# A gated linear attention with an ELU layer: scores, states and values of two half units in two groups of products per unit

## The chip, the core and the metric

The kernel runs on one core of a Trainium2 chip. A core has a matrix engine (TensorE; PE in the profile, PEld for its weight loads), a vector engine (VectorE, DVE), an activation engine (ScalarE, ACT), a general engine (GpSimd, POOL) and a queue that mostly issues transfers (SyncE, SP). [...] The metric is the device time of one execution in microseconds, and lower is better.

## What is computed

A gated linear attention with a complex gate (4 sequences, 8 heads, 768 positions, 48 features per head) is followed by a two-layer network of width 2048 with ELU. All of it is fp32. Cut to what matters:

```python
for t in range(S):                     # S_re, S_im: one D x D state per head
    new_re = ar * S_re - ai * S_im     # ar, ai: the gate, its size capped at 0.999
    new_im = ar * S_im + ai * S_re
    S_re, S_im = new_re + k[t] v[t]^T, new_im
    y[t] = q[t] @ S_re
x = y, heads side by side              # (3072, 384)
h = x @ w_in                           # (3072, 2048)
g = where(h > 0, h, exp(min(h, 0)) - 1)
out = g @ w_out                        # (3072, 384)
```

## The kernel before

**Units.** The work is cut into 12 units. Unit `u` has 128 positions of two sequences; each of the two is a half unit `n`. Units `u` and `u + 2` continue the same two sequences, so states travel from `u` to `u + 2`. A half unit has two chunks `c` of 64 positions.

**Attention of a unit.** Logarithms and angles of the gate are summed along the positions by matmuls (`quartered`, L883, for sizes; `turned`, L832, for angles). Their exponentials, sines and cosines scale `q` and `k` (`gated`, L988). From there, for each half unit:

- `transposed` (L1003, L1004) turns `q` and `k` with TensorE, eight full-size matmuls each, through two banks of tag `w`; ScalarE copies them out to `qt` and `kt`.
- `scores` (L1011, L1016) multiplies `kt` and `qt` of each head and chunk into one `w` bank, and VectorE masks the result into `a`.
- `states` (L1039, L1049, L1051) multiplies `k` and `v` of each head and chunk into a `w` bank per chunk. For each chunk VectorE adds the old state, and GpSimd multiplies by the chunk's decay; the second chunk's sum starts from the first chunk's result.
- `values` (L1061, L1068) multiplies `v` by the masked scores, adds the product of the carried state with `qt`, both into the two-bank tile `y`, and ScalarE copies that to `x` and `y` (L1076, L1080).

`seam` then issues six small transfers from GpSimd's queue (L1093), which move the last rows of `y` into `x`. The products of scores, states and values are small: they fill a part of TensorE's 128x128 array (128x64, 64x64, 128x48 in the profile), several at a time in different places.

**Network of a unit.** `hidden` runs eight times per unit: `inner` (L1113) has twelve matmul instructions of 256 columns into a bank of tag `mlp`; `elu` (L1122 to L1124) needs two ScalarE instructions and one on VectorE. `folded` (L1197) forms sums of `g` on VectorE, four instructions for each half of the hidden width. `product` (L1219) runs 14 times per unit with eight matmul instructions of 192 columns each, into three `mlp` banks, and replaces a plain matmul with `w_out` by seven products of halves.

**PSUM.** Three banks have tag `w`, three have tag `mlp`, and the tile `y` has the last two.

**Order.** The program writes the order of the work itself. `put(at, fn, ...)` gives each step a place `at`; the steps are sorted by it, and steps of equal place stay in the order of the calls, so earlier units come first. Every engine sees its instructions in that one order. With `r = 16 (u - 2)`, these steps surround the change:

| Place | Step |
|---|---|
| r+20 to r+27 | `hidden` 0 to 7 of unit u-1; `folded` of u-1 at r+23 and r+27 |
| r+22 to r+31 | transposes, scores, states, values and seam of unit u |
| r+27 | `squares` (ScalarE, L709, L710), `joined` (GpSimd, L716) of u+1; then `test` (VectorE, L680) |
| r+28 | `logarithms`, `powers` of u+1 (ScalarE, L735 to L747) |
| r+28 to r+35.4 | the 14 products of u-1, 0.57 apart |
| r+29.4, r+29.5 | `lengths` (VectorE, L772), `ratios` (GpSimd, L759, L760) of u+1 |
| r+30.9, r+31 | `slopes` (VectorE, L780), `decays` with `quartered` of u+1 |
| r+31.5, r+32.6, r+34 | `angles` (ScalarE, L815), `carried` (VectorE, L821), `turns` with `turned` (TensorE, L832) of u+1 |

For the units from the fifth on (u of 4 and more), the last row of `values_of`'s places is, for half unit 0: q at r+22, k at r+23, scores at r+24, states at r+25, values at r+27; for half unit 1: q at r+26, k at r+27, scores at r+28, states at r+29, values at r+30; seam at r+31. The first units follow a list that is written out by hand.

Of the kernel before, what the change touches and what calls it, by code (L numbers as in the profile page):

```python
# [10 lines left out]
FP32 = mybir.dt.float32  # L11
U32 = mybir.dt.uint32
AF = mybir.ActivationFunctionType
ALU = mybir.AluOpType
PSUM = bass.MemoryType.PSUM

C = 128
L = 64
# [487 lines left out]
def kernel(  # L506
# [12 lines left out]
    nc = tc.nc  # L519
    B, H, S, D = q.shape  # L520
    DM, DF = moe_w_in.shape[0], moe_w_out.shape[0]
    NI, NF = DM // C, DF // C
    NP = H // 2
    HD = H * D
    NB = 2
    NU = B // NB * (S // C)
    GT = NB * C
# [9 lines left out]
    ps = ctx.enter_context(tc.tile_pool(name="ps", bufs=1, space=PSUM))  # L537
# [10 lines left out]
    def const(n, m, name):  # L548
        return cst.tile([n, m], FP32, name=name)
# [8 lines left out]
    G = HP - D  # L558
# [12 lines left out]
    def work(shape, tag="w"):  # L571
        return ps.tile(shape, FP32, tag=tag, bufs=3, name=tag)


    nat = [{} for _ in range(NU)]

    def where(u):
        return u % (B // NB) * NB, u // (B // NB) * C
# [114 lines left out]
    def new(tag, bufs=1, shape=None):  # L693
        return sb.tile(shape or [C, NB, H, D], FP32, tag=tag, bufs=bufs, name=tag)
# [296 lines left out]
            )  # L991


    state = {}

    def transposed(u, key, n):
        x = nat[u]
        x[key + "t", n] = o = new(key + "t", 1 + (key == "q"), [C, H, C])
        for h0 in range(0, H, 4):
            t = work([C, 4, C])  # L1000
            for h in range(4):
                of = gates[key][:, n, h0 + h].rearrange("p i d -> p (i d)")
                nc.tensor.transpose(t[:, h], of, ident)  # L1003
            nc.scalar.copy(out=o[:, h0 : h0 + 4], in_=t)  # L1004
# [13 lines left out]
        )  # L1018

    def states(u, n):  # L1020

        x = nat[u]
        b, s = where(u)
        x["S", n] = [state.get(b + n)]
        if s == S - C:
            last = C // L - 1
        else:
            last = C // L
        gs = [
            work([C, H, D], "w" if u else "mlp") for c in range(last)  # L1030
        ]
        for h in range(H):
            for c, g in enumerate(gs):
                k = gates["k"][ts(c, L), n, h]
                parts = [(g[ts(i, HP), h], k[:, i]) for i in range(2)]
                if u == 0:
                    parts = [(g[:, h], k.rearrange("p i d -> p (i d)"))]
                for to, of in parts:
                    nc.tensor.matmul(  # L1039
                        to, lhsT=of, rhs=vn[u % 2][ts(c, L), n, ts(h, D)], start=True, stop=True,  # L1040
                    )
        for c, g in enumerate(gs):
            old = x["S", n][-1]
            new_s = new("S", 8, [C, H, D])
            wide = x["T"][:, n, c].unsqueeze(2).to_broadcast([C, H, D])
            if old is None:
                nc.vector.tensor_tensor(out=new_s, in0=g, in1=wide, op=ALU.mult)
            else:
                nc.vector.tensor_tensor(out=new_s, in0=g, in1=old, op=ALU.add)  # L1049
                eng = nc.vector if u < 2 else nc.gpsimd  # L1050
                eng.tensor_tensor(out=new_s, in0=new_s, in1=wide, op=ALU.mult)  # L1051
            x["S", n].append(new_s)
        state[b + n] = x["S", n][-1]

    def values(u, n):
        x = nat[u]
        y = ps.tile([C, C // L, 512], FP32, tag="y", bufs=1, name="y")
        each = [(p, c, j) for p in range(NP) for c in range(C // L) for j in range(2)]
        for p, c, j in each:

            nc.tensor.matmul(  # L1061
                y[ts(j, HP), c, ts(p, L)], lhsT=vn[u % 2][ts(c, L), n, ds((2 * p + j) * D, HP)],
                rhs=x["a", n][ts(c, L), 2 * p + j], start=(p == 0), stop=False,
                skip_group_check=True,
            )
        for p, c, j in each:
            if x["S", n][c] is not None:
                nc.tensor.matmul(  # L1068
                    y[ds(j * HP, D), c, ts(p, L)], lhsT=x["S", n][c][:, 2 * p + j],
                    rhs=x["qt", n][:, 2 * p + j, ts(c, L)], start=False, stop=False,  # L1070
                    skip_group_check=True,
                )
        if n == 0:
            x["x"], x["y"] = new("x", 2, [C, NI, GT]), new("y", 1, [C, GT])

        nc.scalar.copy(  # L1076
            out=x["x"][:, :, ts(n, C)].rearrange("p x (c t) -> p c x t", c=C // L),
            in_=y[:, :, 0 : NI * L].rearrange("p c (x t) -> p c x t", x=NI),
        )
        nc.scalar.copy(  # L1080
            out=x["y"][:, ts(n, C)].rearrange("p (c t) -> p c t", c=C // L),
            in_=y[:, :, NI * L : NP * L],
        )

    def seam(u):
# [167 lines left out]
    def verdict():  # L1253
# [31 lines left out]
        out=ident, in_=ident, pattern=[[-1, C]], base=0, channel_multiplier=1,  # L1285
# [6 lines left out]
    sum_turns, mask = const(C, C, "sum_turns"), const(C, L, "mask")  # L1292
# [14 lines left out]
    parts = [("in", m) for m in range(NF // 2)] + [("out", m) for m in range(NF // WF)]  # L1307
# [20 lines left out]
    def put(at, fn, *args):  # L1328
        if fn is hidden:
            plan.append((at, len(plan), inner, args))  # L1330
            plan.append((at, len(plan), elu, args))
        else:
            plan.append((at, len(plan), fn, args))

    def decays_of(u, *at):
        fns = squares, logarithms, powers, lengths, ratios, slopes, noted, angles, carried
        put(at[0], begun, u)
        for x, fn in zip(at, fns):
            put(x, fn, u)
            if fn is squares:  # L1340
                put(x, joined, u)

    def gates_of(u, *at):
        for x, fn in zip(at, (decays, turns, waves, scaled, ends, gated)):
            put(x, fn, u)

    def values_of(u, *at):
        fns = (transposed, "q"), (transposed, "k"), (scores,), (states,), (values,)
        for n in range(NB):
            for x, (fn, *key) in zip(at[5 * n :], fns):  # L1350
                put(x, fn, u, *key, n)
        put(at[-1], seam, u)
# [12 lines left out]
        (scaled, 0, "k", 1), (scaled, 0, "q", 1), (warm, 1), (gated, 0, 0), (warm, 1), (noted, 0),  # L1365
        (table, "natural_log"), (warm, 2), (gated, 0, 1), (warm, 2), *3 * [(convert,)],
        (transposed, 0, "k", 0), (transposed, 0, "q", 1), (carry_on, 0), (transposed, 0, "q", 0),
        *4 * [(convert,)], (scores, 0, 0), (transposed, 0, "k", 1), (scores, 0, 1), (load_a, 1),
        (squares, 1), (joined, 1), (fetch, "in", 3), (logarithms, 1), (states, 0, 0),
        (values, 0, 0), (powers, 1), (convert,), (states, 0, 1), (lengths, 1), (load_qk, 1),  # L1370
        (convert,), (ratios, 1), (values, 0, 1), (seam, 0), (warm, 2), (warm, 2), (decays, 1),
        (load_a, 2), (warm, 1), (inner, 0, 0), *2 * [(convert,)], (noted, 1), (scaled, 1),
        (warm, 2), (convert,), (load_v, 1), (slopes, 1), (ends, 1), *3 * [(convert,)],
# [43 lines left out]
    def layer_of(u, at_h, at_p):  # L1417
        for m in range(NF // 2):
            put(at_h[m], hidden, u, 2 * m)
        put(at_h[3], folded, u, 0)  # L1420
        put(at_h[7], folded, u, 1)
        ks = [(1, 0), (4, 0), (1, 1), (4, 1)] + [(k, h) for k in (6, 5, 7, 2, 3) for h in range(2)]
        for m, (k, h) in enumerate(ks):
            put(at_p[0] + m * len(at_p) / len(ks), product, u, k, h)

    for u in range(2, NU):
        r = (u - 2) * SLOTS
        put(r + 8, load_a, u)
        put(r + 8, load_v, u)
        put(r + 8, load_qk, u)  # L1430
        if u == 2:
            decays_of(u, 16, 17, 17, 18.4, 19.5, 19.6, 22.7, 19.8, 19.8)
            gates_of(u, 20.4, 21.6, 22.1, 22.4, 22.4, 22.6)
        else:
            decays_of(u, r + 11, r + 12, r + 12, r + 13.4, r + 13.5, r + 14.9, r + 16.7, r + 15.5, r + 16.6)
            gates_of(u, r + 15, r + 18, r + 18.5, r + 18, r + 18, r + 19.5)
        values_of(u, *(max(r + 22, 24.5) + x for x in (0, 1, 2, 3, 5, 4, 5, 6, 7, 8, 9)))
        layer_of(u, range(r + 36, r + 44), range(r + 44, r + 52))
    for m in range(NR):
        put(40 + 4 * m, test_fetch, m)  # L1440
# [42 lines left out]
```

## Time and profile before

| What | Value |
|---|---|
| Time, median of 3 runs | 700.34 us (698.58 to 700.38) |
| Span of the profiled execution, first to last instruction | 700.0 us |
| Busy: TensorE, its weight loads | 674.0 us (96%), 580.5 us (83%) |
| Busy: VectorE, ScalarE, GpSimd | 389.3 us (56%), 398.5 us (57%), 197.3 us (28%) |
| `inner`, all matmuls (L1113) | 262.9 us busy |
| Scores, states (L1011, L1039) | 27.8 us, 25.8 us busy |
| Values, carried part (L1061, L1068) | 17.1 us, 25.1 us busy |
| One unit to the next, by the start of `turned` | 53.5 us (383.7 to 437.2 us) |

The profile shows one execution. Its span lies 0.3 us under the median of the timed runs and inside their spread, so a sum against the span can be read against the median with that shift. [...] neighbours overlap. What a group of matmuls costs is therefore read from its first start to the first start of the next group. A line of the timeline gives start, length, engine, line of code, operation, output and inputs, the part of the array, the shape and the count; in brackets stands the engine's idle time before it and who ended it.

### The profile page before, as it was taken

To read this page: it belongs to the slowest core of one execution; us is meant where nothing else is said; L and a number is where in the kernel's file an instruction comes from. 1 tells how busy PE (TensorE), PEld (TensorE's weight loads), DVE (VectorE), ACT (ScalarE), POOL (GpSimd) and SP (SyncE) were. 2 spreads that over 40 slices of the span, in tenths; PEclk is the share of its full clock that TensorE was granted. 3 is DMA by queue.
4 is the path that set the end of the run, shared out by engine and by line. 5 is a ranking of instruction groups with operands and counts; after the bars stand their busy time and mean duration, and the time that the engine had idled before them with its cause. 6 is when DMAs were issued, how large, how long until landed. Compare 5 with 4: busy or idle time off the path is not lost.

```text
span 700.0 us, 15771 instructions
## 1 busy us (share of the span) xinstructions
PE 674.0 (96%) x6656; PEld 580.5 (83%) x6656; DVE 389.3 (56%) x579; ACT 398.5 (57%) x630; POOL 197.3 (28%) x207
## 2 busy tenths in 40 slices
PE   8799899997999999999999999999999999999996
PEld 6687786575788889888988989889888988989995
DVE  5888999814757544554553553553554644642151
ACT  6774445748656764765655656657557547541230
POOL 2000000115514414414415415406407305402000
PEclk9979999999999999999999999999999999999999
DMA  9995756152082911821921821831731631100000
GB/s 169 175 150 83 144 176 165 17 103 64 3 137 63 143 50 38 138 43 50 136 48 53 123 61 52 121 63 53 108 75 53 123 62 52 47 1 8 23 1 28
DMA packets 149899, 55.98 MB, mean 80 GB/s; under 512 B 129172, under 2 KB 142652, under 8 KB 149820
## 3 DMA queue, kind: packets, MB, share of 16 engines
q1 hardware_dynamic: 146240, 53.53, 40.6%
q0 software_dynamic: 3360, 1.22, 1.3%
q8 instruction: 54, 0.88, 0.5%
q14 instruction: 25, 0.20, 0.1%
q10 hardware_dynamic: 220, 0.14, 0.1%
HBM read 48.88 MB, written 4.78 MB: 77 GB/s over the span
## 4 chain that ended last, share of the span: by engine, by line
PE 85%; DVE 4%; SPq 3%; ACT 2%; DMA 2%; issue 2%; POOL 1%; ACTq 0%; POOLq 0%; DVEq 0%
PE mlp L1113 33%; PE mlp L1219 26%; PE w L1003 5%; PE mlp L1134 4%; PE w L1011 3%; PE y L1068 3%; PE w L1039 3%; SPq L596 2%; PE y L1061 2%; PE w L832 2%; PE w L1134 1%; PE w L883 1%; DMA w<-in_moe_w_in_dram 1%; DMA w<-in_a_im_dram 1%; POOL kg L988 1%
## 5 line engine op out<-in xcount | busy, mean ns | idle before, releaser
L1113 PE MATMUL mlp<-x,w_in 128*128 128x256 f32 x1152 | 262.9, 383 | 2.9 <-DVE g L1124 2.9
L1113 PEld LDWEIGHTS mlp<-x,w_in 128*128 128x128 f32 x1152 | 215.8, 191 | 32.5 <-DVE g L1124 3.3
L1124 DVE SCALAR_TENSOR_TENSOR g<-ee,mlp 128x512 f32<-128x512 f32 x96 | 65.6, 685 | 116.6 <-ACT ee L1123 111.0
L1122 ACT ACTIVATE ee<-mlp 128x512 f32<-128x512 f32 x96 | 57.3, 596 | 127.6 <-PE mlp L1113 118.7
L1219 PE MATMUL mlp<-w_out,g 128*128 128x192 f32 x640 | 111.1, 328 | 0.0
L1219 PEld LDWEIGHTS mlp<-w_out,g 128*128 128x128 f32 x640 | 104.3, 190 | 2.8
L1051 POOL TENSOR_TENSOR S<-S,T 128x384 f32<-128x384 f32 x36 | 29.9, 831 | 163.7 <-DVE S L1049 163.7
L1123 ACT ACTIVATE ee<-ee 128x512 f32<-128x512 f32 x96 | 60.5, 630 | 2.9
L1197 DVE TENSOR_TENSOR g<-g 128x512 f32<-128x512 f32 x80 | 56.8, 711 | 2.7
L1219 PE MATMUL mlp<-w,g 128*128 128x192 f32 x320 | 56.9, 332 | 0.0
L1219 PEld LDWEIGHTS mlp<-w,g 128*128 128x128 f32 x320 | 51.6, 190 | 5.8 <-issue 4.8
L856 POOL DMA_DIRECT2D carry<-n x10 | 5.0, 501 | 142.0 <-DVE n L840 142.0
L988 POOL TENSOR_TENSOR kg<-k,cs 128x1536 f32<-128x1536 f32 x9 | 38.8, 4309 | 18.4 <-issue 18.4
L1093 POOL DMA_DIRECT2D x<-y x65 | 31.8, 496 | 42.7 <-ACT y L1080 42.7
L1049 DVE TENSOR_TENSOR S<-w,S 128x384 f32<-128x384 f32 x38 | 21.1, 556 | 40.7 <-PE w L1039 25.4
L893 ACT ACTIVATE n<-w 64x384 f32<-64x384 f32 (+1 forms) x60 | 28.1, 486 | 22.7 <-PE w L883 22.0
L1238 ACT COPY o<-mlp 128x192 f32<-128x192 f32 x10 | 3.2, 319 | 64.6 <-DMA out_dram<-o 42.9
L716 POOL TENSOR_TENSOR n<-n 128x768 f32<-128x768 f32 x9 | 16.4, 1819 | 66.9 <-ACT n L710 66.9
L1134 PE MATMUL mlp<-w_out,g 128*128 128x384 f32 x96 | 32.9, 490 | 0.7 <-DVE g L1124 0.7
L1004 ACT COPY qt<-w 128x512 f32<-128x512 f32 x48 | 25.5, 584 | 11.9 <-PE w L1003 11.9
L1011 PEld LDWEIGHTS w<-qt,kt 128*64 128x64 f32 x768 | 24.4, 137 | 7.9 <-issue 4.5
L988 DVE TENSOR_TENSOR qg<-q,cs 128x1536 f32<-128x1536 f32 (+1 forms) x12 | 19.5, 1623 | 19.2 <-ACT cs L966 19.2
(165 smaller groups left out, 992.3 us busy)
## 6 DMA issues: line engine op xcount, KB each, us to landing
w<-in_moe_w_out_dram SPq DMA_DIRECT2D x8, 768.0 KB
g<-in_moe_w_in_dram SPq DMA_DIRECT2D x16, 384.0 KB
g<-in_moe_w_out_dram SPq DMA_DIRECT2D x16, 384.0 KB
w<-in_moe_w_in_dram SPq DMA_DIRECT2D x16, 288.0 KB
vn<-in_v_dram SPq DMA_DIRECT2D x24, 192.0 KB
out_dram<-o SPq DMA_DIRECT2D x48, 96.0 KB
ar<-in_a_re_dram SPq DMA_DIRECT2D x22, 192.0 KB
ai<-in_a_im_dram SPq DMA_DIRECT2D x22, 192.0 KB
```

The source lines that it names most:

```text
L988: eng.tensor_tensor(out=to[:, :, :, 0:D], in0=each.unsqueeze(2).to_broadcast([C, step * H, 2, D]), in1=x["cs"][:, n * H : (n + step) * H], ...
L1003: nc.tensor.transpose(t[:, h], of, ident)
L1011: nc.tensor.matmul(t[ts(c, L), h], lhsT=x["kt", n][:, h, ts(c, L)], rhs=x["qt", n][:, h, ts(c, L)], start=True, stop=True,)
L1051: eng.tensor_tensor(out=new_s, in0=new_s, in1=wide, op=ALU.mult)
L1093: eng.dma_start(out=x["x"][ds(j * HP + D, G), i], in_=x["y"][ds(j * HP + i * G, G)])
L1113: nc.tensor.matmul(t[:, e], lhsT=w_in[:, i, ts(f + e, C)], rhs=x["x"][:, i], start=(i == 0), stop=(i == NI - 1),)
L1122: nc.scalar.activation(out=e, in_=t, func=AF.Relu, scale=-1.0)
L1123: nc.scalar.activation(out=e, in_=e, func=AF.Exp, scale=-1.0)
L1124: nc.vector.scalar_tensor_tensor(out=x["g", f // 8][:, f % 8 : f % 8 + 2], in0=e, scalar=-1.0, in1=t, op0=ALU.add, op1=ALU.max)
L1134: nc.tensor.matmul(x["o", n], lhsT=x["g", f // 8][:, f % 8, ts(n, C)], rhs=w_out[:, f], start=(f == 0), stop=(f == NF - 1),)
L1197: nc.vector.tensor_tensor(out=S_of(u, k, h), in0=a, in1=b, op=op)
L1219: nc.tensor.matmul(to, lhsT=a[:, m], rhs=b[:, m], start=(first and h == 0 and m == 0), stop=False, skip_group_check=True,)
```

## The change

From the fifth unit on, the six separate steps (scores, states, values, for two half units) become two. `states` is split into `state_products` (TensorE) and `state_sums` (VectorE and GpSimd), and `values` into `value_products`, `carried_products` and `value_copies`. The first four units keep the old order.

- `scored`, at r+26.6: the state products of half unit 0, then the scores of both half units into a tile of tag `y` (one bank for each half unit), then the sums of half unit 0 and the two masks, alternating.
- `valued`, at r+29.3: the state products of half unit 1, the value products of both half units into one tile `y` (the half units side by side in each chunk's bank), the sums of half unit 1, the carried products of both half units sorted by chunk, and three copies in place of four.
- `seam` follows at r+29.3. The transposes stand at r+22 (q, 0), r+23 (k, 0), r+24 (q, 1) and r+25.3 (k, 1). The second `kt` lies in the buffer of tag `cs`.

```diff
+    PAIRED = 4
     def transposed(u, key, n):
         x = nat[u]
-        x[key + "t", n] = o = new(key + "t", 1 + (key == "q"), [C, H, C])
+        if u >= PAIRED and key == "k" and n:
+            o = new("cs", 1, [C, H, C])
+        else:
+            o = new(key + "t", 1 + (key == "q"), [C, H, C])
+        x[key + "t", n] = o
...
+    def carried_products(u, n, y):
+        x = nat[u]
+        for p, c, j in EACH if u < PAIRED else sorted(EACH, key=lambda x: x[1]):
...
+    def scored(u):
+
+        x = nat[u]
+        state_products(u, 0)
+        t = ps.tile([C, NB, 512], FP32, tag="y", bufs=1, name="y")
+        for n in range(NB):
+            for h in range(H):
+                for c in range(C // L):
+                    nc.tensor.matmul(
+                        t[ts(c, L), n, ts(h, L)], lhsT=x["kt", n][:, h, ts(c, L)],
+                        rhs=x["qt", n][:, h, ts(c, L)], start=True, stop=True,
+                    )
+        for n in range(NB):
+            state_sums(u, 0, [n])
+            x["a", n] = new("a", 2, [C, H, L])
+            nc.vector.tensor_tensor(
+                out=x["a", n], in0=t[:, n].rearrange("p (h t) -> p h t", h=H),
+                in1=mask.unsqueeze(1).to_broadcast([C, H, L]), op=ALU.mult,
+            )
+
+    def valued(u):
+
+        x = nat[u]
+        y = ps.tile([C, C // L, 512], FP32, tag="y", bufs=1, name="y")
+        state_products(u, 1)
+        for n in range(NB):
+            value_products(u, n, y[:, :, ts(n, NP * L)], n == 0)
+        state_sums(u, 1)
+        for n in range(NB):
+            carried_products(u, n, y[:, :, ts(n, NP * L)])
+        x["x"], x["y"] = new("x", 2, [C, NI, GT]), new("y", 1, [C, GT])
+        parts = y.rearrange("p c (n x t) -> p c n x t", n=NB, x=NP)
+        to = x["x"].rearrange("p x (n c t) -> p c n x t", n=NB, c=C // L)
+        for c in range(C // L):
+            nc.scalar.copy(out=to[:, c], in_=parts[:, c, :, 0:NI])
+        nc.scalar.copy(
+            out=x["y"].rearrange("p (n c t) -> p c n t", n=NB, c=C // L), in_=parts[:, :, :, NI],
         )
...
-        values_of(u, *(max(r + 22, 24.5) + x for x in (0, 1, 2, 3, 5, 4, 5, 6, 7, 8, 9)))
+        if u < PAIRED:
+            values_of(u, *(max(r + 22, 24.5) + x for x in (0, 1, 2, 3, 5, 4, 5, 6, 7, 8, 9)))
+        else:
+            for n in range(NB):
+                put(r + 22 + 2 * n, transposed, u, "q", n)
+                put(r + 23 + 2.3 * n, transposed, u, "k", n)
+            put(r + 26.6, scored, u)
+            put(r + 29.3, valued, u)
+            put(r + 29.3, seam, u)
```

More of the change, by code (lines that the diff above doesn't have):

```diff
@@ L1020, in states, with state_products @@
     def states(u, n):
+        state_products(u, n)
+        state_sums(u, n)
+    def state_products(u, n):
         x = nat[u]
@@ L1028, in states @@
             last = C // L
-        gs = [
+        x["G", n] = gs = [
             work([C, H, D], "w" if u else "mlp") for c in range(last)
@@ L1041, in states, with state_sums @@
                     )
-        for c, g in enumerate(gs):
+    def state_sums(u, n, chunks=range(C // L)):
+        x = nat[u]
+        for c, g in list(enumerate(x["G", n])):
+            if c not in chunks:
+                continue
             old = x["S", n][-1]
@@ L1052, in states, with value_products @@
             x["S", n].append(new_s)
-        state[b + n] = x["S", n][-1]
+        state[where(u)[0] + n] = x["S", n][-1]
     def values(u, n):
+        y = ps.tile([C, C // L, 512], FP32, tag="y", bufs=1, name="y")
+        value_products(u, n, y)
+        carried_products(u, n, y)
+        value_copies(u, n, y)
+    EACH = [(p, c, j) for p in range(NP) for c in range(C // L) for j in range(2)]
+    def value_products(u, n, y, first=True):
         x = nat[u]
-        y = ps.tile([C, C // L, 512], FP32, tag="y", bufs=1, name="y")
-        each = [(p, c, j) for p in range(NP) for c in range(C // L) for j in range(2)]
-        for p, c, j in each:
+        for p, c, j in EACH:
             nc.tensor.matmul(
                 y[ts(j, HP), c, ts(p, L)], lhsT=vn[u % 2][ts(c, L), n, ds((2 * p + j) * D, HP)],
-                rhs=x["a", n][ts(c, L), 2 * p + j], start=(p == 0), stop=False,
+                rhs=x["a", n][ts(c, L), 2 * p + j], start=(first and p == 0), stop=False,
                 skip_group_check=True,
             )
-        for p, c, j in each:
+    def carried_products(u, n, y):
+        x = nat[u]
+        for p, c, j in EACH if u < PAIRED else sorted(EACH, key=lambda x: x[1]):
             if x["S", n][c] is not None:
@@ L1072, in values, with value_copies @@
                 )
+    def value_copies(u, n, y):
+        x = nat[u]
         if n == 0:
@@ L1082, in values @@
             in_=y[:, :, NI * L : NP * L],
+        )
+    def scored(u):
+        x = nat[u]
+        state_products(u, 0)
[13 more added lines that the diff above has]
+                in1=mask.unsqueeze(1).to_broadcast([C, H, L]), op=ALU.mult,
+            )
+    def valued(u):
+        x = nat[u]
+        y = ps.tile([C, C // L, 512], FP32, tag="y", bufs=1, name="y")
+        state_products(u, 1)
[11 more added lines that the diff above has]
+            out=x["y"].rearrange("p (n c t) -> p c n t", n=NB, c=C // L), in_=parts[:, :, :, NI],
         )
```

## The prediction

> **What bounds the kernel.** I read the page first: its busy shares, then its chain by engine.
>
> ```profile
> PE 674.0 (96%) x6656; PEld 580.5 (83%) x6656; DVE 389.3 (56%) x579; ACT 398.5 (57%) x630; POOL 197.3 (28%) x207
> ...
> PE 85%; DVE 4%; SPq 3%; ACT 2%; DMA 2%; issue 2%; POOL 1%; ACTq 0%; POOLq 0%; DVEq 0%
> ```
>
> TensorE is never long idle, and it carries 85% of the chain. So a microsecond taken out of its order is worth one, unless something new makes it wait. Next comes its timeline in one steady unit.
>
> ```profile
> 414.91 0.69 PE L1061 MATMUL y<-a,vn 64*64 64x64 f32 x32
> 415.53 1.10 PE L1068 MATMUL y<-qt,S 128*48 128x64 f32 x32
> 416.56 1.09 PE L1003 MATMUL w<-ident,kg 128*128 128x128 f32 x8
> 417.50 1.47 PE L1219 MATMUL mlp<-w_out,g 128*128 128x192 f32 x8
> 418.89 1.15 PE L1011 MATMUL w<-qt,kt 128*64 128x64 f32 x32
> 419.97 1.57 PE L1219 MATMUL mlp<-wt,g 128*128 128x192 f32 x8
> 421.47 1.15 PE L1039 MATMUL w<-vn,kg 64*64 64x48 f32 x64
> 422.55 1.57 PE L1219 MATMUL mlp<-w_out,g 128*128 128x192 f32 x8
> 423.95 1.46 PE L1219 MATMUL mlp<-wt,g 128*128 128x192 f32 x8
> ...
> 433.31 4.06 PE L1219 MATMUL mlp<-w_out,g 128*128 128x192 f32 x24
> 437.21 1.45 PE L832 MATMUL w<-n,sum_turns 128*128 128x384 f32 x4
> ```
>
> From start to start, eight product matmuls take 1.30 us with no small group beside them (24 in 3.90), 1.39 before a small group (417.50), 1.40 after one (422.55), 1.50 between two (419.97). Each border costs about 0.1. Inside a small group single starts run evenly, 58 ns for two scores, so 32 should take 0.93; they take 1.08, with 0.05 lost at the first pair and 0.10 at the end. Third, VectorE and GpSimd around the change:
>
> ```profile
> 206.71 7.14 DVE L1197 TENSOR_TENSOR g<-g 128x512 f32<-128x512 f32 x8
> 208.67 1.84 POOL L716 TENSOR_TENSOR n<-n 128x768 f32<-128x768 f32 x1 [4.84 <-ACT n L710]
> ...
> 417.03 2.87 DVE L1197 TENSOR_TENSOR g<-g 128x512 f32<-128x512 f32 x4
> 419.82 0.55 DVE L680 TENSOR_REDUCE seen<-g 128x1 f32<-128x384 f32 x1
> 419.88 1.82 POOL L716 TENSOR_TENSOR n<-n 128x768 f32<-128x768 f32 x1 [7.34 <-ACT n L710]
> 425.75 2.36 POOL L759 TENSOR_TENSOR n<-ar,n 128x768 f32<-128x768 f32 x1
> 428.19 1.81 POOL L760 TENSOR_TENSOR n<-ai,n 128x768 f32<-128x768 f32 x1
> 429.94 2.94 POOL L1093 DMA_DIRECT2D x<-y  x6
> 430.25 0.95 DVE L780 SCALAR_TENSOR_TENSOR n<-n 128x768 f32<-128x768 f32 x1
> ```
>
> Four folds take 2.87 alone at 417.03; eight, with the join (L716) among them, take 7.14 and not 5.74: the join held them up by 1.40. In the steady units the join begins when the last fold ends. The seam (L1093) stands behind both ratios (L759, L760) on GpSimd.
>
> [...] 0.15 between the last value product and the first carried one, where the mode changes, against 0.06 inside. [...] the seam in L1093 starts only after L760. [...] a fold that starts at 208.87 lasts 2.19 instead of 0.70 while the join runs, and gets done 0.54 after it.
>
> **Step 1, the switches of TensorE.** Entering a small group costs 0.09, its first pair 0.05 (0.035 for states), leaving it 0.10, the next full matmuls 0.10 (0.06 for transposes); a change of mode inside costs 0.11 + 0.04. Before, a unit pays: scores 0.34 twice, states 0.34 twice, values 0.45 (with transposes behind) and 0.49: 2.31. After: states with scores 0.49; states with values (both 64x64, no change of mode) and carried 0.48; together 0.97. The transposes of half unit 1 move between two `inner` and pay nothing. Saved: 1.35 a unit, 8 units, −10.8 us. The matmuls themselves are the same; if states to values cost a mode change after all, it is 0.15 less.
>
> **Step 2, buffers, at nothing.** The score tile needs `y` free: its last copies lie 20 us back. The value tile needs both masks: they end 5 us before it. The state products need two `w` banks, freed by adds as far back. `cs` is read by `gated` before the transposes begin. The cover is the work between the two groups, one `inner` (2.7) and three products (3.9); without it each mask or add (0.6 to 0.7) would be paid. The chunks' state sums of half unit 0 have the same cover. ScalarE has three copies, two of 0.48 and one between 0.27 and 0.48, for 1.50 before; not on the path.
>
> **Step 3, the join meets the folds.** I count from the first matmul of the first product behind the eighth `inner` (time 0). The eighth Relu starts at 0.20 (0.41 after the last `inner` matmul's start), folds at 2.22 (Relu 415.01, folds 417.03). Before, ScalarE copied values and `kt` (1.8 us) between this ELU and the squares; now these copies are gone, so the squares run at once: from 1.35, ready at 2.93, join asked for at 3.0, amid the folds (2.22 to 5.1). [...] The folds are 1.40 later, the reduce (L680) starts at 6.41, the add of half unit 1, chunk 0 at 6.87, GpSimd's multiply at 7.51; it ends at 8.34, and TensorE sees it near 8.44. Who waits is the carried product of half unit 1, chunk 1. TensorE gets there at: products 3.90 + 0.09, state products 0.93 + 0.04, value products 0.90, mode 0.15, 24 pairs of carried products 1.38, so 7.39. Wait 1.05. Behind it stand all of TensorE's products. Without the delay the multiply would be seen at 7.04, 0.35 early. It happens in units 4 to 10 (unit 11 has no successor to join): 7 × 1.05 = +7.4 us. Bounds: −0.35 hidden, so 0, if the two miss each other[...].
>
> **Step 4, the seam moves ahead of the ratios.** GpSimd's order is now multiplies, six seam transfers, ratios. The join ends at 5.30; logarithm and two exponentials take 3.81 from 5.38 (421.87 to 425.68), so 9.19; copies to 10.4; seam 2.94 to 13.4; ratios 3.75 to 17.15; slopes 1.03, Arctan 0.87, carried 0.98: 20.03; `turned` can start at 20.13. TensorE reaches it at 19.44 without step 3's wait, and at 20.48 with it. So the seam costs 0.7 a unit where step 3 costs nothing, and nothing on top of it; the dearer of the two counts. Behind `slopes` VectorE holds a reduce, `carried` and the product's adds; TensorE needs those adds 0.3 us after they end.
>
> **Sum.** 700.0 − 10.8 + 7.4 = 696.6 against the profiled span; the median lies 0.3 above it. **697.0 us.**
>
> **Rivals.**
>
> - **Clean:** no wait at either place, 700.3 − 10.8 = 689.5. For: the reckoned lateness is 1.05 and 0.7 out of 20 us of summed rows. Against: both queues are regular from unit to unit, and both must come out early. 10%.
> - **Only the seam counts:** join and folds miss each other or cost less, 0.7 a unit, 694.4. 18%.
> - **Slower[...]:** the four folds run to 5.1 before the join gets in. The join then ends near 6.8, the logarithm 1.5 later, and with copies, seam and ratios `turned` is ready at 21.6, 2.1 late: 7 × 2.1 − 10.8 = +3.9, 704.2. It decides from a wait of 1.54 a unit on (10.8 / 7). Against: at 208.67 the join got in after one fold. 15%.
> - **The switches stay:** states, scores and carried each still pay as a group of their own because the mode changes inside. Then only the two half units' merging saves, near 1.0 a unit, and with the waits it is 700. 7%.
>
> **Chances.** My forecast, a wait of 0.9 to 1.5 a unit (696 to 700): 50%. This kernel's measurement can tell 0.3% (2.1 us) from no change; that bound is at a wait of 1.24. Of the 50%, 32 lie under it. Faster: 32 + 18 + 10 = 60%. Within: 18 + 7 = 25%. Slower: 15%. The range leaves out half of the clean case and most of the slower one: waits of 0.45 and 1.85, 692.5 to 702.5. The forecast's own range is 696 to 700.
>
> **What would show it.** Step 1: between `inner` 7 and the next group no small products; one group from first state to last score in about 3.1 us. Step 3: L716 beginning inside the folds, a fold of about 2.2, and a gap before L1068 inside the carried products, released by GpSimd's L1051. Step 4: L1093 ahead of L759, and L832 waiting on VectorE's L821 or not. I am wrong if carried products don't wait, if `turned` waits longer than they do, or if the groups don't shrink TensorE's span between two `turned` from 53.5 to about 53.2.

## The result, and the profile after

Changed kernel: 700.49 us (median of 20 runs, 697.89 to 702.57). Kernel before, on the same chip: 700.36 us (median of 20 runs, 698.13 to 703.67). The ratio is 0.9997, with a 95% interval from 0.9984 to 1.0009: no difference that this measurement can tell. The profiled span is 699.0 us, against 700.0 us.

The page of the changed kernel, busy shares and chain by engine:

```profile
PE 665.2 (95%) x6656; PEld 580.0 (83%) x6656; DVE 399.6 (57%) x579; ACT 397.5 (57%) x622; POOL 201.6 (29%) x207
...
PE 72%; DVE 11%; ACT 7%; POOL 5%; issue 3%; DMA 1%; ACTq 1%; POOLq 0%; DVEq 0%
```

TensorE is busy for 8.8 us less, but the chain that ended last leaves it more often: 72% instead of 85%, with VectorE at 11% instead of 4% and GpSimd at 5% instead of 1%. The same matmuls take less time, and TensorE now waits for others.

Where it waits is seen in the timeline. First the group with the scores in unit 7, and the folds and the join behind it (start, length, engine, line, operation, shape, count):

```profile
408.97 1.15 PE L1048 MATMUL w<-vn,kg 64*64 64x48 f32 x64
410.05 1.15 PE L1118 MATMUL y<-qt,kt 128*64 128x64 f32 x32
...
412.07 2.86 PE L1177 MATMUL mlp<-x,w_in 128*128 128x256 f32 x12
416.98 4.37 DVE L1261 TENSOR_TENSOR g<-g 128x512 f32<-128x512 f32 x4
417.76 2.31 POOL L716 TENSOR_TENSOR n<-n 128x768 f32<-128x768 f32 x1 [3.45 <-ACT n L710]
```

States and scores of two half units are one group of 3.10 us (408.97 to 412.07), as forecast. The join (L716) begins 0.78 us after the first fold; four folds take 4.37 us instead of 2.87. What follows from that, in unit 8:

```profile
474.05 1.55 PE L1090 MATMUL y<-qt,S 128*48 128x64 f32 x48
475.62 0.83 POOL L1065 TENSOR_TENSOR S<-S,T 128x384 f32<-128x384 f32 x1 [2.28 <-DVE S L1063]
476.50 0.65 PE L1090 MATMUL y<-qt,S 128*48 128x64 f32 x16 [0.90 <-POOL S L1065]
```

The carried products stop after 48 of 64 instructions, until GpSimd's multiply (L1065) has ended. From the start of the 48th to that of the 49th it is 1.12 us, where the usual step from pair to pair is 0.05. From the first carried product to the next group it is 3.04 us here, and 1.92 in a later kernel without this wait: the halt costs 1.12 a unit. In units 5, 7 and 9 a part of it comes earlier, after 28, 31 and 34 instructions, with no releaser in the profile. Such stops come up again below; in units 7 and 9 they fall into time that TensorE would have waited anyway, and only in unit 5 is the whole longer, 3.20 us.

The last stretch is unit 9's end and the sizes and angles of unit 10:

```profile
536.85 1.81 POOL L760 TENSOR_TENSOR n<-ai,n 128x768 f32<-128x768 f32 x1
537.77 0.48 ACT L893 ACTIVATE n<-w 64x384 f32<-64x384 f32 x1
538.61 1.81 POOL L976 TENSOR_TENSOR k<-k,n 128x768 f32<-128x768 f32 x1
538.69 2.55 DVE L780 SCALAR_TENSOR_TENSOR n<-n 128x768 f32<-128x768 f32 x1 [3.70 <-POOL n L760]
...
543.24 1.53 PE L832 MATMUL w<-n,sum_turns 128*128 128x384 f32 x4 [1.21 <-DVE n L821]
```

This was not forecast. Scaling `k` (L976) needs the last exponentials (L893), which end at 538.25, and the ratios end after them, at 538.66. So GpSimd goes on from the ratios to L976 at once. VectorE's `slopes` (L780) starts 0.08 us after L976 and takes 2.55 us, where 0.95 is usual. Arctan, `carried` and `turned` follow it, and `turned` comes 1.21 us late. In the kernel before, the same stretch is:

```profile
536.92 2.94 POOL L1093 DMA_DIRECT2D x<-y  x6
...
540.65 1.80 POOL L976 TENSOR_TENSOR k<-k,n 128x768 f32<-128x768 f32 x1 [0.80 <-ACT n L893]
```

The ratios ended at 536.97, and `slopes` (at 537.23, 0.95 us) was done at 538.18. L976 still had to wait for the last exponentials when the seam was over, for another 0.80 us. So the two could not meet. With the seam ahead of them the ratios come so late that the exponentials are there first. The view of all waits of the changed kernel (us in total, times, longest) has it twice:

```profile
PE w L832 <- DVE n L821: 2.4, 2, 1.2
```

These are the periods that end with `turned` of units 10 and 11. In the kernel before, L832 never waits for L821.

The periods from one unit's `turned` to the next one's, in us, read off the first L832 of each:

| `turned` of unit | 4 to 5 | 5 to 6 | 6 to 7 | 7 to 8 | 8 to 9 | 9 to 10 | 10 to 11 |
|---|---|---|---|---|---|---|---|
| before | 53.48 | 53.49 | 53.49 | 53.49 | 53.49 | 53.49 | 53.46 |
| after | 53.27 | 53.43 | 53.27 | 53.27 | 53.26 | 54.65 | 54.72 |

The account, from `turned` of unit 4 to the end:

| Term | us |
|---|---|
| switches of TensorE, 8 × 1.35 (as step 1 reckoned it) | −10.8 |
| halt of the carried products, 7 × 1.12 | +7.8 |
| `slopes` behind L976, (54.65 + 54.72 − 2 × 53.27) | +2.8 |
| one stop of TensorE in unit 5 (53.43 − 53.27) | +0.2 |
| sum | 0.0 |

Measured over that stretch: 476.7 us before, 476.9 after. The span is shorter by 1.0 all the same, because this execution reached `turned` of unit 4 1.2 us earlier (222.08 against 223.27), in code that the change doesn't touch.

### The profile page after: what moved, and what is told of

It reads as the page before. It is cut to its first block, busy times and chain, and to the rows that moved or that the text cites. A ratio compares the mean times of both kernels' runs of the same rounds, so it can differ in the third digit from the quotient of the medians.

```text
span 699.0 us, 15744 instructions
## 1 busy us (share of the span) xinstructions
PE 665.2 (95%) x6656; PEld 580.0 (83%) x6656; DVE 399.6 (57%) x579; ACT 397.5 (57%) x622; POOL 201.6 (29%) x207
## 4 chain that ended last, share of the span: by engine, by line
PE 72%; DVE 11%; ACT 7%; POOL 5%; issue 3%; DMA 1%; ACTq 1%; POOLq 0%; DVEq 0%
PE mlp L1177 32%; PE mlp L1283 19%; PE w L1008 6%; DVE g L1261 3%; PE y L1118 2%; PE w L1048 2%; PE mlp L1198 2%; PE w L832 2%; PE y L1090 2%; DVE n L780 1%; DVE g L1188 1%; POOL S L1065 1%; PE w L1016 1%; DVE wf L43 1%; PE mlp L1386 1%
## 5 line engine op out<-in xcount | busy, mean ns | idle before, releaser
L1283 PE MATMUL mlp<-w_out,g 128*128 128x192 f32 x640 | 110.3, 326 | 0.0
L1283 PEld LDWEIGHTS mlp<-w_out,g 128*128 128x128 f32 x640 | 105.4, 190 | 2.7
L1065 POOL TENSOR_TENSOR S<-S,T 128x384 f32<-128x384 f32 x36 | 33.7, 936 | 192.0 <-DVE S L1063 192.0
L1261 DVE TENSOR_TENSOR g<-g 128x512 f32<-128x512 f32 x80 | 67.3, 842 | 2.7
L1283 PEld LDWEIGHTS mlp<-w,g 128*128 128x128 f32 x320 | 52.0, 190 | 5.1 <-issue 4.8
L1283 PE MATMUL mlp<-w,g 128*128 128x192 f32 x320 | 56.0, 329 | 0.0
L856 POOL DMA_DIRECT2D carry<-n x10 | 5.3, 525 | 137.4 <-DVE n L840 137.4
L893 ACT ACTIVATE n<-w 64x384 f32<-64x384 f32 (+1 forms) x60 | 28.1, 486 | 27.8 <-PE w L883 27.1
L780 DVE SCALAR_TENSOR_TENSOR n<-n 128x768 f32<-128x768 f32 x11 | 13.7, 1247 | 35.7 <-POOL n L760 35.7
L716 POOL TENSOR_TENSOR n<-n 128x768 f32<-128x768 f32 x9 | 19.8, 2197 | 40.1 <-ACT n L710 40.1
L1090 PE MATMUL y<-qt,S 128*48 128x64 f32 x704 | 25.0, 222 | 6.0 <-POOL S L1065 4.1
```

What stands on the lines that cost most here:

```text
L1090: nc.tensor.matmul(y[ds(j * HP, D), c, ts(p, L)], lhsT=x["S", n][c][:, 2 * p + j], rhs=x["qt", n][:, 2 * p + j, ts(c, L)], start=False, st ...
L1261: nc.vector.tensor_tensor(out=S_of(u, k, h), in0=a, in1=b, op=op)
L1283: nc.tensor.matmul(to, lhsT=a[:, m], rhs=b[:, m], start=(first and h == 0 and m == 0), stop=False, skip_group_check=True,)
```

## The experiments

Three questions: is the new 2.8 us really the scaling of `k` beside `slopes`, is the carried wait really the join beside the folds, and is step 1's saving all there once both are gone? The theory says yes to all three. The rivals: the seam's earlier place is what delays the angles; the carried wait comes from some other lateness of the adds; the switches saved less than reckoned. All ratios are to the kernel before, on the same chip.

### The seam behind the ratios

```diff
-            put(r + 29.3, seam, u)
+            put(r + 29.6, seam, u)
```

> The changed kernel with one edit: the seam stands behind the ratios again (r+29.6 instead of r+29.3). Theory [...]: in the changed kernel the angles' matmuls of units 10 and 11 came 1.2 us late because GpSimd went from the ratios straight to the scaling of k[...]. With six seam transfers between the two[...]: the last two periods fall from 54.7 to 53.3 us, 2.8 us in all, a ratio to the kernel before near 0.996. The other periods stay at 53.3, since there the carried product waits for VectorE's late add, not for the seam. Rival (the seam's place costs in every unit): all periods fall by 0.7 or more, the ratio goes to 0.992 or lower. Rival (the last two units are slow for their own reason, one chunk less): nothing changes, 1.000.

Measured: 698.07 us, ratio 0.9964 (0.9950 to 0.9978). The periods are 53.27, 53.27, 53.27, 53.28, 53.27, 53.28, 53.25: the last two have lost their excess, and the other five haven't moved, except that the stop in unit 5 no longer lengthens its period. The stretch of unit 10:

```profile
536.40 2.94 POOL L1157 DMA_DIRECT2D x<-y  x6
536.50 0.96 DVE L780 SCALAR_TENSOR_TENSOR n<-n 128x768 f32<-128x768 f32 x1 [0.56 <-POOL n L760]
538.71 0.48 ACT L893 ACTIVATE n<-w 64x384 f32<-64x384 f32 x1
539.36 1.82 POOL L976 TENSOR_TENSOR k<-k,n 128x768 f32<-128x768 f32 x1
```

The ratios end at 536.46, and `slopes` is over at 537.46. L976 can't begin before the last exponentials, at 539.19. So it is the earlier ratios that keep the two apart, and not, as the expectation had it, the transfers between them. In the stretch of unit 11 this is plain: the transfers end at 591.35, and L976 still waits for the exponentials.

```profile
592.53 1.81 POOL L976 TENSOR_TENSOR k<-k,n 128x768 f32<-128x768 f32 x1 [1.18 <-ACT n L893]
```

Behind the carried wait, the seam's place costs nothing in units 4 to 9: step 4 had that right. What it missed is whom the late ratios meet.

### The scaling of k behind other transfers, in the last two units

Units 10 and 11 hand no state to a later unit, so two transfers (L946) can go ahead of their scaling:

```diff
-            gates_of(u, r + 15, r + 18, r + 18.5, r + 18, r + 18, r + 19.5)
+            gates_of(u, r + 15, r + 18, r + 18.5, r + 18 + 0.1 * (u >= NU - 2), r + 18, r + 19.5)
```

> The changed kernel with one edit, in units 10 and 11 alone: GpSimd's two transfers of the chunk decays stand ahead of the scaling of k, so that GpSimd waits for the round trip of those decays before it scales. Theory [...]: the slopes of these two units last 0.95 us again instead of 2.55, the matmul of the angles waits for nothing, and the last two periods fall from 54.7 to 53.3; 2.8 us, ratio near 0.996. Rival (the last two units are slow for another reason, or the seam ahead of the ratios is enough to make them late): the periods stay at 54.7, 1.000.

Measured: 700.12 us, ratio 0.9997 (0.9979 to 1.0014). The gain expected for the whole, 2.8 us, is missed. The period to unit 10 is cured (53.28), the one to unit 11 is worse: 55.33. The two together are 0.8 us shorter than in the changed kernel.

```profile
591.89 3.21 DVE L821 SCALAR_TENSOR_TENSOR n<-carry,n 1x768 f32<-1x768 f32 x1 [0.45 <-ACT n L815]
592.47 1.81 POOL L976 TENSOR_TENSOR k<-k,n 128x768 f32<-128x768 f32 x1
595.25 1.53 PE L832 MATMUL w<-n,sum_turns 128*128 128x384 f32 x4 [1.91 <-DVE n L821]
```

Put off by a transfer that waits, L976 lands on `carried` (L821) instead: 3.21 us where 0.95 is usual, and `turned` waits 1.91. The culprit is the same, the victim another. The seam stands where the changed kernel has it, and the period to unit 10 is cured all the same. So the late ratios alone cost nothing there; the loss comes with L976 beside an instruction of VectorE.

### The second group later

`valued` goes behind the sizes of the next unit, and so the adds have 1 us more; the seam stays ahead of the ratios.

```diff
-            put(r + 29.3, valued, u)
-            put(r + 29.3, seam, u)
+            put(r + 29.75, valued, u)
+            put(r + 29.82, seam, u)
```

with `lengths` at r+29.8 and `ratios` at r+29.85 for units from 5 on (r of the unit before).

> The changed kernel with the second group one product later (behind four products instead of three), lengths and ratios of the next unit moved behind it, the seam still ahead of the ratios. Theory: the carried product of half unit 1, chunk 1 comes 1.3 us later and no longer waits (its wait was 1.07), so nothing hides the seam any more: the matmul of the angles waits 0.7 us in five units and 2.3 in the last two[...]. Periods 52.9 and 54.5; 8 x 1.35 saved less 5 x 0.7 and 2 x 2.3: 2.7 us under the kernel before, ratio 0.996. Rival (the wait of the carried product was all that cost): periods 52.1, ratio 0.985. Rival (switches were not saved): periods 53.5 or more, 1.000 or over.

Measured: 703.12 us, ratio 1.0049 (1.0026 to 1.0073): slower, where a gain was expected.

```profile
373.97 2.94 POOL L1157 DMA_DIRECT2D x<-y  x6 [0.24 <-ACT y L1145]
...
383.64 1.53 PE L832 MATMUL w<-n,sum_turns 128*128 128x384 f32 x4 [0.68 <-DVE n L821]
```

The carried wait is gone: its 64 instructions run through, at 370.49 in unit 6 with 1.99 us in one piece. But the seam, which waits for the copies of `y`, now starts later and holds the ratios back, and `turned` waits in every unit, with 0.68 us of idle time in the records. This is step 4's seam, which step 3's wait had covered. It was reckoned at 0.7 a unit; in the period it is 0.9 (53.25, against 52.33 in the next run). The period is 53.18 to 53.25 in four units. The last two pay 1.6 us each for L976 beside `slopes` (L780 takes 2.54 and 2.55 there, against 0.96 at 380.68), and stops of TensorE add 1.2 and 0.6 in two units. So the expectation failed on the whole: taking one wait away showed the next.

### Both: the second group later, the seam behind the ratios

```diff
+            put(r + 29.75, valued, u)
+            put(r + 29.9, seam, u)
```

with `lengths` and `ratios` as in the run before.

> As the run with the late second group, but with the seam behind the ratios. Theory: neither wait is left and the scaling of k does not meet the slopes; what remains is what the fewer switches save, 1.35 us a unit: periods 52.1 us instead of 53.5, 8 x 1.35 = 10.8 us, 689.6, ratio 0.985. Rival (the switches save less than reckoned, because the mode changes inside a group[...]): periods 52.5 to 53.5, ratio 0.989 to 1.000.

Measured: 694.16 us, ratio 0.9910 (0.9885 to 0.9934). Five periods are 52.33, and two are 53.27 and 52.90. Reckoned was 53.49 − 1.35 = 52.14, so 0.19 a unit was missing. In the timeline of unit 6:

```profile
369.12 1.99 PE L1090 MATMUL y<-qt,S 128*48 128x64 f32 x64
370.88 0.30 ACT L1291 COPY ee<-mlp 128x192 f32<-128x192 f32 x1
371.23 2.87 PE L1283 MATMUL mlp<-w,g 128*128 128x192 f32 x16
```

The next product starts 2.11 us after the first carried one. It writes the bank that ScalarE's copy (L1291) still reads until 371.18; the view of waits has TensorE's weight loads of L1283 wait for L1291 five times, 1.3 us in all. The other two periods hold a stop of TensorE for which the profile shows no releaser, here in unit 7, after 23 of the 64 instructions:

```profile
423.19 1.37 PE L1090 MATMUL y<-qt,S 128*48 128x64 f32 x41 [0.87 <-issue]
```

### Another product first, behind the second group

The kernel just shown, with the order of two products exchanged:

```diff
-        ks = [...] + [(k, h) for k in (6, 5, 7, 2, 3) for h in range(2)]
+        ks = [...] + [(k, h) for k in (5, 6, 7, 2, 3) for h in range(2)]
```

> As the run with both waits gone (e4), with the products of the network in another order: the two of k = 5 ahead of the two of k = 6. In e4 the period is 52.33, 0.19 over the reckoned 52.14, and the exit from the second group lasts 0.33 us instead of 0.15. Theory: the first product behind it, k = 6, writes the PSUM bank that ScalarE's copy of k = 1 still reads, and that copy stands behind the exponentials; k = 5 opens a bank of its own. Exit 0.15, periods 52.15 [...], 1.2 us less than e4 in all, ratio near 0.989. Rival (the longer exit is a price of the longer group): exit and period stay at 0.33 and 52.33.

Measured: 691.14 us, ratio 0.9875 (0.9851 to 0.9900). It is the lowest median of all and beats both kernels; from the run before (0.9885 to 0.9934) the intervals don't part it.

```profile
365.63 1.99 PE L1090 MATMUL y<-qt,S 128*48 128x64 f32 x64
367.55 2.87 PE L1283 MATMUL mlp<-w,g 128*128 128x192 f32 x16
```

From the first carried product to the next group it is 1.92 us, 0.19 less, and the row of waits for L1291 is gone. Five periods are 52.13 to 52.15; two are 52.97 and 52.83, with the stops still there. 53.49 − 52.15 = 1.34 a unit: with nothing in its way, step 1's saving is what it was reckoned to be. The step is shown by the periods, not by the whole: in this profile the end behind the last `turned` is 2.0 us longer than in the run before (102.71 against 100.71), with TensorE waiting 1.25 us for VectorE there, and how far the timed runs share that is not known.

### The join on VectorE

With the seam behind the ratios, and the carried products where the changed kernel has them:

```diff
-            products(u).tensor_tensor(out=x["m2"], in0=x["m2"], in1=x["sq"], op=ALU.add)
+            nc.vector.tensor_tensor(out=x["m2"], in0=x["m2"], in1=x["sq"], op=ALU.add)
```

> As the run with the seam behind the ratios (e1), with the join of squares on VectorE, behind the folds, instead of GpSimd. VectorE so gets 0.95 us more to do ahead of the add. Theory [...]: the folds take 2.87 us again instead of 4.37, so the add comes 0.45 earlier all the same; the carried product waits 0.6 instead of 1.07, periods 52.8 instead of 53.3, ratio near 0.992. Rival (VectorE's queue was simply full[...]): the add comes 0.95 later, periods 54.2, ratio 1.003.

Measured: 696.46 us, ratio 0.9941 (0.9920 to 0.9963).

```profile
417.95 2.87 DVE L1261 TENSOR_TENSOR g<-g 128x512 f32<-128x512 f32 x4
420.73 0.95 DVE L716 TENSOR_TENSOR n<-n 128x768 f32<-128x768 f32 x1
```

Without the join on GpSimd four folds take 2.87 us again: they were slow only beside it. (The join's own 0.95 is VectorE's time and doesn't compare with GpSimd's 2.31; on GpSimd with no fold beside it, in the kernel before, it took 1.82.) The add still stands behind the join, but starts 6.33 us after the first product behind the eighth `inner` instead of 6.96, so 0.63 earlier. The gap in the carried products shrinks by the same amount, from 1.13 to 0.50. The period is 52.97, not 52.8: 0.3 of the 0.63 goes to the wait for ScalarE's copy again, now at the second product behind the group, since the carried products leave earlier.

### The reduce ahead of the adds twice

VectorE's reduce (L680), which stands ahead of the add, is issued a second time in the step ahead of that add, in units 4 to 10:

```diff
+        for _ in range(1 + (m >= 4 and m % 4 == 0)):
             nc.vector.tensor_reduce(
```

> The changed kernel, with the reduce that stands between the folds and the add of half unit 1 done twice (same input, same output), 0.55 us more on VectorE in each unit. Theory (the carried product waits for this add, through GpSimd's multiply): its wait grows by 0.47, periods 53.7 instead of 53.3 in units 4 to 9; the last two periods stay at 54.7, since there the late angles take up the difference: 2.4 us more, ratio near 1.003. Rival (VectorE is 57% busy and off TensorE's path): nothing changes, 1.000.

Measured: 705.41 us, ratio 1.0067 (1.0043 to 1.0091). The same rows in unit 7, whose line numbers are one higher:

```profile
426.37 0.83 POOL L1066 TENSOR_TENSOR S<-S,T 128x384 f32<-128x384 f32 x1 [2.87 <-DVE S L1064]
427.25 0.65 PE L1091 MATMUL y<-qt,S 128*48 128x64 f32 x16 [0.92 <-POOL S L1066]
```

GpSimd waits 2.87 us for the add instead of 2.28, and the period grows by 0.58 (53.85), all that the second reduce adds (1.13 for two, 0.55 for one). So the add sets the end of the unit one for one, and no slack is left before it. The whole was underestimated. The last two periods grew too, by 0.5 each (55.14 and 55.23): copies, seam and ratios follow the carried products, so that the late `slopes` of these units does not hide behind the carried wait but comes on top of it.

### Another hundred instructions on TensorE

To see what the stops hang on, the kernel of the second group later and the seam behind the ratios gets 100 more TensorE instructions at its start, matmuls of its step `warm`:

```diff
-        (warm, 1), (warm, 12), (fetch, "in", 0), ...
+        (warm, 1), (warm, 37), (fetch, "in", 0), ...
```

> As e4, with 25 more warming matmuls at the very start (some 100 TensorE instructions), which compute nothing that is used. In e4 TensorE stands still for 1.08 and 0.65 us inside the carried products of units 7 and 9, at the same counts of its instructions as in four other kernels, 256 x 9 apart. Theory [...]: the stops move with the count; none in units 7 and 9, some of up to 1.1 us in units 4, 6, 8 or 10[...]. Rival (something in units 7 and 9 makes TensorE wait): the stops stay. The time itself decides nothing here: the start may be longer by up to 5 us.

Measured: 696.28 us, ratio 0.9957 (0.9941 to 0.9973). The stops left the carried products of units 7 and 9 and appear in units 4, 6 and 8, where the step over the stop takes 0.62, 0.38 and 0.46 us. (The period to unit 10 is 52.60 for another reason: L976 lies beside `carried`, which takes 1.54 us.) Unit 7 now:

```profile
421.70 1.99 PE L1090 MATMUL y<-qt,S 128*48 128x64 f32 x64
```

Counted along TensorE's rows in the trace (weight loads included), up to the last matmul ahead of the stop, the stops of the other kernels fall behind numbers 6081, 8385 and 10689, each 9 × 256 after the last; here behind 5057, 7361 and 9665, also 9 × 256 apart. The two sets are 1024 = 4 × 256 apart, so that all six leave 193 when divided by 256. So a stop belongs to a place in the instruction stream. All that can be seen lie in carried products. Ahead of the stop in unit 7 of the kernel without the hundred, the trace has a transfer of the kind `instruction` (from 420.47, 1.17 us long), over about 0.5 us before the stop begins. Such transfers run through the whole execution (the view of transfers counts 79 packets), most of them with no stop near. That TensorE waits for them is not shown. Nor do the runs say why a stop's length varies from nothing that can be seen in the period (unit 5 of the kernel without the hundred) to 1.2 us. The timed runs are slower than these periods would make them (367.6 us from `turned` of unit 4 to that of unit 11, 367.8 without the hundred). The profiled execution was the fastest of the twelve, and what the others spend was not followed up.

## Why the prediction was wrong

It forecast 697.0 us, 3.3 us under the time before, with 60% for faster. Measured were 700.5 us, which can't be told from the time before: 3.5 us more than forecast. By its steps:

- **Step 1, the switches: right.** Forecast 1.35 us a unit, measured 1.34 in the kernel with both waits gone. The group with the scores takes 3.10 us, and TensorE reaches the first carried product 6.02 us after the products begin, with 6.01 reckoned. In unit 8 of the changed kernel the first value product starts 0.04 us after the last state product (both 64x64), as inside a group, and the first carried one 0.15 after the last value product. The rival in which the switches stay is out. What the step did not have is the stops inside the long groups: 0.8 and 0.7 us in two units of the fastest kernel, none in the periods of the kernel before.
- **Step 2, buffers at nothing: right for the changed kernel.** No mask, add or score tile holds TensorE. But its cover doesn't reach to what comes behind the second group: once the carried wait is gone, ScalarE's copy of product 1 costs 0.19 a unit there. The carried wait hid that.
- **Step 3, join against folds: cause right, size short by 0.07.** Forecast 1.05 a unit, measured 1.12, of which 1.07 is the wait and the rest a slower restart: 7 × 0.07 = 0.5 us of the error. The join is asked for at 3.00, as reckoned; it holds the folds up by 1.50 instead of 1.40. The join got in amid the folds, 0.78 us after the first one, and four folds take 4.37 us with it on GpSimd and 2.87 with it on VectorE. What the two engines share is not shown. The rival in which all four folds run ahead of the join is out.
- **Step 4, the seam: the step that failed.** It reckoned how late the seam makes the ratios, priced `slopes` behind them at 1.03, and put the whole behind step 3's wait, "nothing on top of it". For units 4 to 9 this holds: moving the seam back alters no period there, and taking step 3's wait away brings the seam's cost out (0.68 of idle time before `turned`). For units 10 and 11 the price of `slopes` was wrong: it took 2.55 us, beside the scaling of `k` (L976), which the step left out. The late ratios end after the last exponentials, so L976 is ready when they end and follows at once. In the earlier units the transfer of the carry (L856) stands between, which waits for VectorE's L840 and so until after `turned` (8.10 us of idle time, up to 440.22, in the changed kernel's unit 8). The last two have no unit to carry to. That is +2.8 us in two units, and the last two periods of the kernel with two reduces show that it adds to step 3's wait rather than hiding behind it.
- **The sum.** −10.8 + 7.4 was forecast; the runs give −10.8 + 7.8 + 2.8 + 0.2. Of the 3.5 us, 2.8 is step 4, 0.5 step 3, 0.2 a stop of TensorE.
- **The rivals.** None held the cause. They let join and seam cost more or less, in every unit alike; a cost in the units where the pipeline ends was in none. The forecast also had little room: 697.0 lay 3.3 us under the time before, and 2.1 us can't be told from nothing, so that 1.2 us of cost in any place was enough to decide it. 60% for faster was too much for a sum of two large terms of opposite sign.

What stays open is the stop of TensorE, as said, and how much of it an order of the instructions could avoid.

## What to carry to other kernels

When a step makes an in-order queue late, ask not only who waits for the late result. Ask also what stands behind it in the same queue, whether that will be ready by then, and which instruction of another engine it will then run beside: two steps that one wait kept apart can so come to lie beside each other. Look at the units at the end of the pipeline by themselves, since an instruction that held others back may be missing there. And when a saving on the bounding engine is eaten by waits, take them out one after the other until the period falls by what was reckoned: here three lay behind each other (the add, the seam, a copy's bank), and without them, with two products exchanged as well, the change is worth 1.25% (0.9875, 0.9851 to 0.9900).

## What the runs showed of the hardware

- **Instructions of VectorE and GpSimd that ran beside each other were recorded longer, on either engine.** `slopes` took 2.55 us instead of 0.95 beside L976, `carried` 3.21 instead of 0.95, four folds 4.37 instead of 2.87 beside the join, and the join 2.31 instead of 1.82. No row of waits names it: it is found by comparing one line's length in two units. Not all were: VectorE's reduce (L680) took 0.55 us beside L976 too (at 440.71 in the changed kernel). What the engines share there is not shown.
- **GpSimd took seam and ratios in the order of the program.** In the kernel before, ScalarE's copies of `y` had ended at 427.76 us, and the seam began at 429.94, when the second ratio (428.19 to 430.00) was ending. In the changed kernel `lengths`, which the ratios need, had ended at 424.64, and the first ratio began at 428.40, when the seam (425.47 to 428.39) was over.
- **In these runs TensorE stopped at places of its own instruction stream.** The step over a stop took 0.4 to 1.3 us, against 0.05 as a rule. All stops seen lie in carried products, behind instruction numbers that differ by multiples of 256 (2304 and 1024), and a hundred added instructions moved them to other units. What TensorE waits for there is open.
